# A block for rows beyond the experts' room, moved to the end of the program with a second pass of the MLP

## The chip, the core and the metric

The kernel runs on one core of a Trainium2 chip. A core has TensorE (PE, matmuls; its weight loads are listed as PEld), VectorE (DVE), ScalarE (ACT), GpSimd (POOL) and SyncE (SP), each with its own queue of instructions and its own sequencer, which handles register loads, branches and waits on semaphores. The metric is the device time of one execution in microseconds; of several runs the median counts.

## What is computed

Sliding-window attention, then a mixture of experts with one expert per token and a capacity, then a second MLP over all 1152 tokens:

```python
x = attention(q, k, v)                      # 2 x 576 tokens, 8 heads of 64, window of 64
x = x.transpose(0, 2, 1, 3).reshape(1152, 512)
# experts: token i goes to argmax(x @ w_gate), as long as that expert has room (288)
h = np.maximum(np.einsum('ecd,edf->ecf', disp, w1), 0.0)      # 8 experts, 512 -> 1024
y = np.einsum('ecf,efd->ecd', h, w2)                          # 1024 -> 512
x = gate_w * y[expert, pos]                                   # 0 where the expert was full
# second MLP
h = x @ w_in                                                  # 512 -> 2048
g = np.maximum(h, 0.0) + alpha * np.minimum(h, 0.0)
out = g @ w_out                                               # 2048 -> 512
```

## The kernel before

The kernel is written engine by engine in a fixed order (`tc.manual_schedule()`): what the program lists first on an engine stands first in its queue, and the framework adds the semaphore waits. All tensors of the matmuls are split into a high and a low part, and three matmuls (high x high, high x low, low x high) make one product (`mm3`, L185 to L188).

It has three stages. Attention, routing and the scatter of the rows by expert come first. Then the experts are worked off in an order that depends on how many rows each got: the rows lie sorted in `xs` (two tiles, high and low, 512 features as 4 blocks of 128 by 1152 + 256 columns), an expert of rank 1 to 3 gets a window of 256 rows (`wide_up`, `wide_down`), the others 128 (`narrow`), and the results go to `x2`, which is laid out like `xs`. The last expert is a wide one; its `wide_down` finishes the four feature blocks one after the other, and for each, `put(d)` has ScalarE write the high and VectorE the low part of that block of `x2` (L937, L938). The third stage is the second MLP, in four quarters `qq`. A quarter has 12 calls of `up` (each 12 matmuls of 384 columns into a tile `gps`, L188; ScalarE makes `u`, VectorE `g`, and both split it into `gh` and `gl`) and 9 of `down` (each 12 matmuls of 512 columns into `ops`, L1212, added to `acc` by ScalarE or VectorE). In the last quarter every `down` ends with a scatter of its 128 rows to `out` by GpSimd (L1220). The weights of this MLP come in through SyncE's queue (L92), in 32 pieces, and are converted and split by ScalarE and VectorE (`cvt_tick`), some of it ahead of the MLP, during the last expert.

Where an expert got more rows than its window holds, the rest is worked off between the experts and the second MLP. `n_over`, the number of such rows, is read into a register on every engine (L1098), and `with tc.If(n_over > 0)` (L1099) opens the block: it clears windows of `x2`, then holds for each of the eight experts a further `If` (L1120) with the whole of its two layers for the remaining rows. With the inputs of the runs shown `n_over` is 0, and all engines jump over the block. On TensorE the block is some 2370 of 4843 listed instructions. Behind the block, `over.close()` (L1160) gives the memory of `xs` free, and the pools of the second MLP open.

A `tc.If` has a branch for true and one for false on every engine. The false branch holds only semaphore steps, by which each engine's counters are raised to where the true branch would have left them, so that what stands behind the `If` can wait on one count in both cases.

The lines that touch the edge, as they stand:

```python
n_over = nc.values_load(inci[0:1, NS + 2 * NE:NS + 2 * NE + 1], min_val=0, max_val=NT)   # L1098
with tc.If(n_over > 0):                                                                    # L1099
    ...                                                                                    # L1101 to L1159
over.close()                                                                               # L1160
with ExitStack() as es:                                                                    # L1163, the second MLP
```

Of the kernel before, what the change touches and what calls it, by code (L numbers as in the profile page):

```python
# [27 lines left out]
def attention_moe_mlp_kernel(  # L28
# [145 lines left out]
    scattered, written = [], []  # L174
# [15 lines left out]
    with tc.manual_schedule():  # L190
# [905 lines left out]


        n_over = nc.values_load(inci[0:1, NS + 2 * NE:NS + 2 * NE + 1], min_val=0, max_val=NT)  # L1098
        with tc.If(n_over > 0):  # L1099
# [60 lines left out]
        over.close()  # L1160


        with ExitStack() as es:  # L1163
            accp = es.enter_context(tc.tile_pool(name="accp", bufs=1))
            gtp = es.enter_context(tc.tile_pool(name="gtp", bufs=4 * NTB))
            tmp = es.enter_context(tc.tile_pool(name="tmp", bufs=3))
            ps_h = es.enter_context(tc.tile_pool(name="ps_h2", bufs=4, space=PSUM))
            ps_o = es.enter_context(tc.tile_pool(name="ps_o", bufs=4, space=PSUM))
            acc = accp.tile([128, NTILE, D], F32, name="acc")
            base = 8 * NE  # L1170
            gts, unsplit = {}, []

            def need(c):
                while cvt_n[0] < 2 * (c - n_moe) + 3:
                    cvt_tick(c)

            def up(qq, c, tb, f):
                cs, fs = slice(TB * tb, TB * tb + TB), slice(128 * f, 128 * f + 128)
                ft = 4 * qq + 2 * c + f
                hi, lo = (w.rearrange("p (k f) -> p k f", k=4) for w in parts[base + 4 * qq + c])  # L1180
                need(base + 4 * qq + c)
                ps = ps_h.tile([128, TB], F32, name="gps", tag="g")
                for kk in range(4):
                    mm3(ps, (hi[:, kk, fs], lo[:, kk, fs]), (x2[0][:, kk, cs], x2[1][:, kk, cs]), kk == 0, kk == 3)
                u = tmp.tile([128, TB], F32, name="u", tag="u")
                g = tmp.tile([128, TB], F32, name="g", tag="gf")

                nc.scalar.activation(out=u, in_=ps, func=AF.Copy, scale=one[:, ft:ft + 1])  # L1188
                nc.vector.scalar_tensor_tensor(g, ps, slope[:, ft:ft + 1], u, op0=ALU.mult, op1=ALU.max)  # L1189
                split()  # L1190
                unsplit.append((tb, 2 * c + f, sign[:, ft:ft + 1], g))

            def split():

                while unsplit:
                    tb, f, sg, g = unsplit.pop()
                    gh = gtp.tile([128, TB], F32R, name="gh", tag="gh")
                    gl = gtp.tile([128, TB], F32R, name="gl", tag="gl")
                    nc.scalar.activation(out=gh, in_=g, func=AF.Copy, scale=sg)  # L1199
                    nc.vector.scalar_tensor_tensor(gl, g, sg, gh.bitcast(F32), op0=ALU.mult, op1=ALU.subtract)  # L1200
                    gts[tb, f] = (gh, gl)

            def down(qq, tt):
                tb, t = divmod(tt, TB // 128)
                ts_ = slice(128 * t, 128 * t + 128)
                need(base + 4 * qq + 3)
                ps = ps_o.tile([128, D], F32, name="ops", tag="o")
                for f in range(4):
                    hi, lo = (w.rearrange("p (k f) -> p k f", k=2) for w in parts[base + 4 * qq + 2 + f // 2])
                    gh, gl = gts[tb, f]  # L1210
                    for n, (a_, b_) in enumerate(((gh, hi), (gh, lo), (gl, hi))):
                        nc.tensor.matmul(ps, a_[:, ts_], b_[:, f % 2, :], start=f == 0 and n == 0,  # L1212
                                         stop=f == 3 and n == 2)
                sc = gate[:, tt:tt + 1]
                if qq == 0:
                    nc.scalar.mul(acc[:, tt, :], ps, sc)
                else:
                    nc.vector.scalar_tensor_tensor(acc[:, tt, :], ps, sc, acc[:, tt, :], op0=ALU.mult, op1=ALU.add)  # L1218
                if qq == NQ - 1:
                    ins = nc.gpsimd.indirect_dma_start(  # L1220
                        out=out[:, :],
                        out_offset=bass.IndirectOffsetOnAxis(ap=tok[:, tt:tt + 1].bitcast(U32), axis=0),
                        in_=acc[:, tt, :], in_offset=None)
                    apart(written, ins)


            sign, one, slope = (accp.tile([128, 16], F32, name=x) for x in ("sign", "one", "slope"))
            nc.vector.tensor_scalar(sign, al, 1.0, -2.0, op0=ALU.is_gt, op1=ALU.mult)
            nc.vector.tensor_scalar(sign, sign, 1.0, None, op0=ALU.add)
            nc.vector.tensor_scalar(one, sign, 1 / UP, None, op0=ALU.mult)  # L1230
            nc.vector.tensor_tensor(slope, one, al, op=ALU.mult)
            gate = accp.tile([128, NTILE], F32, name="gate")
            nc.vector.tensor_scalar(gate, gt[:, :, 1], 1 / UP, None, op0=ALU.mult)
            done = base - 1
# [57 lines left out]
```

## Time and profile before

| | us |
|---|---|
| median of 3 runs | 432.46 (432.07 to 435.01) |
| the profiled execution | 438.73 |
| its span, first to last instruction of the program | 437.0 |
| TensorE busy (matmuls) | 413.6 |
| VectorE busy | 322.6 |
| ScalarE busy | 225.9 |
| GpSimd busy | 62.8 |

Rows of the timeline give the start and the length in us, engine, line, operation and tiles, and in brackets the idle time ahead of the instruction and what ended it. A q behind an engine's name (PEq, DVEq, PEldq) is its sequencer: such steps occupy no engine. [...] In the rows of one line the three times after the count are shortest, median and longest, in ns, and behind them stand the starts of the first and the last, in us.

### The profile page before, as it was taken

The page shows a single profiled execution, that of the slowest core. Times are in us where ns is not written, and L with a number is a line of the kernel's source. Part 1 is how long each engine was busy: PE and PEld are TensorE (multiplying, and loading weights), DVE is VectorE, ACT ScalarE, POOL GpSimd, SP SyncE. Part 2 cuts the span into 40 slices and gives each one's busy share as a digit, 9 for nine tenths or more (in the row PEclk, how much of TensorE's full clock was granted, in tenths as well). Part 3 has the DMA queues.
Part 4 walks back from the last instruction along what each step waited for, and adds up shares of the span by engine and source line. Part 5 has one row for each costly group of instructions (what it writes and reads, how often), then busy time and mean ns, then how long its engine had stood idle before and what let it go on. Part 6 is the DMA issues. An engine that isn't in the chain of part 4 may idle for free. (4 is left out here: it accounts for less than half of the span.)

```text
span 437.0 us, 7987 instructions
## 1 busy us (share of the span) xinstructions
PE 413.6 (95%) x2707; PEld 374.4 (86%) x2707; DVE 322.6 (74%) x755; ACT 225.9 (52%) x474; POOL 62.8 (14%) x109
## 2 busy tenths in 40 slices
PE   7899979889999999999969999999999999999994
PEld 4789867578998899988969998899889998899883
DVE  3998958758988878877963996699994996245421
ACT  3887836455647654755533675577532770045200
POOL 8433535850000000000000000000000000000132
PEclk9999969999999999999996999999999999999998
DMA  7999676976698768788740345344341100000122
GB/s 254 303 355 382 209 244 243 371 208 187 211 316 262 247 239 303 231 273 284 230 164 4 103 137 145 96 145 115 128 144 48 49 0 1 0 2 0 37 99 82
DMA packets 27857, 74.90 MB, mean 171 GB/s; under 512 B 3041, under 2 KB 8161, under 8 KB 27809
## 3 DMA queue, kind: packets, MB, share of 16 engines
q1 hardware_dynamic: 25648, 67.08, 46.7%
q0 software_dynamic: 2160, 7.23, 4.6%
q8 instruction: 24, 0.39, 0.4%
q14 instruction: 25, 0.20, 0.2%
HBM read 62.75 MB, written 11.55 MB: 170 GB/s over the span
## 5 line engine op out<-in xcount | busy, mean ns | idle before, releaser
L106 DVE TENSOR_TENSOR wlo<-raw,whi 128x1024 fp32r<-128x1024 f32 x60 | 72.2, 1222 | 8.3 <-ACT whi L897 7.2
L188 PE MATMUL gps<-x2h,whi 128*128 128x384 f32 x192 | 65.5, 341 | 4.5 <-DVEq L1099 4.5
L188 PE MATMUL gps<-x2h,wlo 128*128 128x384 f32 x192 | 65.3, 340 | 0.0
L188 PE MATMUL gps<-x2l,whi 128*128 128x384 f32 x192 | 65.3, 340 | 0.0
L1188 ACT ACTIVATE u<-gps,one 128x384 f32<-128x384 f32 x48 | 27.7, 576 | 62.7 <-PE gps L188 62.7
L1212 PE MATMUL ops<-whi,gl 128*128 128x512 f32 x144 | 56.1, 390 | 0.0
L1212 PE MATMUL ops<-wlo,gh 128*128 128x512 f32 x144 | 56.1, 390 | 0.0
L1220 POOL DMA_INDIRECT out<-acc,tok x9 | 8.7, 965 | 329.4 <-DVE acc L1218 329.4
L1212 PE MATMUL ops<-whi,gh 128*128 128x512 f32 x144 | 56.0, 389 | 0.0
L897 ACT CAST whi<-raw 128x1024 fp32r<-128x1024 f32 x42 | 43.4, 1050 | 10.7 <-PE y L188 5.4
L1189 DVE SCALAR_TENSOR_TENSOR g<-gps,slope,u 128x384 f32<-128x384 f32 x48 | 29.5, 614 | 22.6 <-ACT u L1188 22.5
L1218 DVE SCALAR_TENSOR_TENSOR acc<-ops,gate,acc 128x512 f32<-128x512 f32 x27 | 20.0, 748 | 30.6 <-PE ops L1212 30.6
L188 PEld LDWEIGHTS gps<-x2h,whi 128*128 128x128 f32 x192 | 37.0, 193 | 4.8 <-ACTq L1099 4.6
L188 PEld LDWEIGHTS gps<-x2l,whi 128*128 128x128 f32 x192 | 36.9, 192 | 0.1
L188 PEld LDWEIGHTS gps<-x2h,wlo 128*128 128x128 f32 x192 | 36.9, 192 | 0.0
L1199 ACT ACTIVATE gh<-g,sign 128x384 fp32r<-128x384 f32 x48 | 29.3, 610 | 9.3 <-DVE g L1189 9.3
L371 ACT ACTIVATE pt<-ms,nm 128x128 f32<-128x128 f32 x72 | 28.0, 391 | 8.4 <-DVE nm L361 7.3
L1212 PEld LDWEIGHTS ops<-whi,gl 128*128 128x128 f32 x144 | 27.0, 188 | 5.6
L1212 PEld LDWEIGHTS ops<-wlo,gh 128*128 128x128 f32 x144 | 27.0, 188 | 5.6
L1212 PEld LDWEIGHTS ops<-whi,gh 128*128 128x128 f32 x144 | 27.0, 188 | 5.5
L1200 DVE SCALAR_TENSOR_TENSOR gl<-g,sign,gh 128x384 fp32r<-128x384 f32 x48 | 29.3, 610 | 0.2 <-ACT gh L1199 0.2
L158 DVE TENSOR_TENSOR wlo<-w,whi 128x512 fp32r<-128x512 f32 x32 | 22.0, 687 | 8.0 <-ACT whi L157 7.8
(247 smaller groups left out, 947.3 us busy)
## 6 DMA issues: line engine op xcount, KB each, us to landing
raw<-moe_in SPq DMA_DIRECT2D x61, 512.0 KB, 5.0
raw<-mlp_in SPq DMA_DIRECT2D x32, 512.0 KB, 3.6
xe<-zr SPq DMA_DIRECT2D x1, 6600.0 KB
v<-v_in SPq DMA_DIRECT2D x8, 512.0 KB
sw<-moe_in SPq DMA_DIRECT2D x4, 512.0 KB
qT<-q_in SPq DMA_DIRECT2D x4, 384.0 KB
kT<-k_in SPq DMA_DIRECT2D x4, 384.0 KB, 7.1
qT<-q_in SPq DMA_DIRECT2D x1, 768.0 KB, 9.5
```

Of the source, the lines that this page charges most:

```text
L106: eng.tensor_tensor(lo, raws.pop(c), hi.bitcast(F32), op=ALU.subtract)
L158: nc.vector.tensor_tensor(lo, w, hi.bitcast(F32), op=ALU.subtract)
L188: nc.tensor.matmul(ps, wa[i], xa[j], start=start and n == 0, stop=stop and n == 2)
L371: nc.scalar.activation(out=pt[:, p, :], in_=sc[:, p, :], func=AF.Exp, scale=-1.0, bias=nm[:, p:p + 1], accum_out=ss[:, p:p + 1])
L897: (nc.vector.tensor_copy if c % 4 == 3 else nc.scalar.copy)(ring_tiles(c)[0], raws[c])
L1188: nc.scalar.activation(out=u, in_=ps, func=AF.Copy, scale=one[:, ft:ft + 1])
L1189: nc.vector.scalar_tensor_tensor(g, ps, slope[:, ft:ft + 1], u, op0=ALU.mult, op1=ALU.max)
L1199: nc.scalar.activation(out=gh, in_=g, func=AF.Copy, scale=sg)
L1200: nc.vector.scalar_tensor_tensor(gl, g, sg, gh.bitcast(F32), op0=ALU.mult, op1=ALU.subtract)
L1212: nc.tensor.matmul(ps, a_[:, ts_], b_[:, f % 2, :], start=f == 0 and n == 0, stop=f == 3 and n == 2)
L1218: nc.vector.scalar_tensor_tensor(acc[:, tt, :], ps, sc, acc[:, tt, :], op0=ALU.mult, op1=ALU.add)
L1220: ins = nc.gpsimd.indirect_dma_start(out=out[:, :], out_offset=bass.IndirectOffsetOnAxis(ap=tok[:, tt:tt + 1].bitcast(U32), axis=0), in_=a ...
```

## The change

The block moves to the end of the program. `over.close()` comes directly behind the experts; the code of the second MLP becomes a function, `second_mlp`, that is called once in the place of the old code, and then once more as the last thing in the `If`, for the case that rows are left over. Since `xs` is gone by then, the block first gathers the rows again into two new tiles. The `If` gets `preferred_fallthrough_block=False`: the false branch stands directly behind the compare-and-branch in the program, and ends with an unconditional jump past the true branch to the program's closing barrier. Inside `up`, `need` is called ahead of looking the weights up, which in the first pass issues the same instructions.

```diff
-    scattered, written = [], []
+    scattered = []
...
                 else:
                     narrow(p, wins[p], xts.pop(p))
 
+        over.close()
+
+
+        def second_mlp():
+            written = []
+            with ExitStack() as es:
+                accp = es.enter_context(tc.tile_pool(name="accp", bufs=1))
...
+                def up(qq, c, tb, f):
+                    cs, fs = slice(TB * tb, TB * tb + TB), slice(128 * f, 128 * f + 128)
+                    ft = 4 * qq + 2 * c + f
+                    need(base + 4 * qq + c)
+                    hi, lo = (w.rearrange("p (k f) -> p k f", k=4) for w in parts[base + 4 * qq + c])
...
+        second_mlp()
+
+
 
         n_over = nc.values_load(inci[0:1, NS + 2 * NE:NS + 2 * NE + 1], min_val=0, max_val=NT)
-        with tc.If(n_over > 0):
+        with tc.If(n_over > 0, preferred_fallthrough_block=False):
+            over = ExitStack()
+            xsp = over.enter_context(tc.tile_pool(name="xsp2", bufs=1))
+            xs = [xsp.tile([128, 4, XW], F32R, name=f"xo{n}") for n in "hl"]
+            with ExitStack() as es:
+                gp = es.enter_context(tc.tile_pool(name="gp2", bufs=2))
+                ps_x = es.enter_context(tc.tile_pool(name="ps_x2", bufs=2, space=PSUM))
...
+                for j in range(NTILE):
+                    xg = gp.tile([128, ROW], F32, name="xgo", tag="xgo")
+                    nc.gpsimd.indirect_dma_start(
+                        out=xg, out_offset=None, in_=xe[:, :],
+                        in_offset=bass.IndirectOffsetOnAxis(ap=ixi[:, j:j + 1].bitcast(U32), axis=0))
...
             with ExitStack() as es:
                 zp = es.enter_context(tc.tile_pool(name="zp", bufs=1))
...
-        over.close()
-
-
-        with ExitStack() as es:
-            accp = es.enter_context(tc.tile_pool(name="accp", bufs=1))
...
+            over.close()
+            cvt_n[0] = 0
+            parts.clear()
+            for c in range(NRAW):
+                load(n_moe + c)
+            second_mlp()
```

On TensorE, before, this stands at the edge from the last matmuls of the experts (`y`, from the split hidden values `hh`, `hl` and the weights `whi`, `wlo`) to the block; in brackets are the semaphores that a row waits for, named after the engine or queue that raises them:

```order
L188 MATMUL y_3181<-hh,whi 128x256
L188 MATMUL y_3181<-hl,whi 128x256
L188 MATMUL y_3181<-hh,wlo 128x256
L1098 TENSOR_LOAD inci [waits DVE_49]
L1099 COMPARE_AND_BRANCH
L1111 TENSOR_LOAD at_z [waits DVE_49,PE_49,Activation_49]
```

And behind the block, where the second MLP begins with `gps`:

```order
L1120 UNCONDITIONAL_BRANCH [waits PE_49,PE_sequencer_49]
L1099 UNCONDITIONAL_BRANCH [waits PE_49,PE_sequencer_49]
L188 MATMUL gps<-x2h,whi 128x384 [waits DVE_49,PE_49,Activation_49]
L188 MATMUL gps<-x2l,whi 128x384
L188 MATMUL gps<-x2h,wlo 128x384
```

There the first matmul waits for three counts, those that the engines raise in the `If`. In the changed kernel the same place of TensorE reads as follows; the four feature blocks of the first `gps` repeat the three rows shown, each with its own two waits:

```order
L188 MATMUL y_3181<-hl,whi 128x256
L188 MATMUL y_3181<-hh,wlo 128x256
L188 MATMUL gps<-x2h,whi 128x384 [waits Activation_49]
L188 MATMUL gps<-x2l,whi 128x384 [waits DVE_49]
L188 MATMUL gps<-x2h,wlo 128x384
L188 MATMUL gps<-x2h,whi 128x384 [waits Activation_49]
```

The load and the branch are gone from between `y` and `gps`, and the counts waited for are those of the writes of `x2` by ScalarE (L937) and VectorE (L938), block by block. On all five engines the rows up to the end of the second MLP are otherwise the old ones in the old order.

GpSimd, before, reaches the `If` right behind its fills of `xs`, early in the expert stage. It passes over 25 listed rows, to the row of L1099 behind which the scatters stand:

```order
L1085 MEMSET xsl 128x4x256
L1098 TENSOR_LOAD inci [waits DVE_49]
L1099 COMPARE_AND_BRANCH
L1106 IOTA atf 128x9 [waits DVE_49,PE_49,Activation_49]
L1119 TENSOR_LOAD inci
```

In the changed kernel the `If` stands behind GpSimd's last scatter. The last rows of its way are these (`DMASW` are the semaphores that the scatters' transfers raise on landing; the row called ISA adds to them what the true branch would have added):

```order
L1159 DMA out<-acc,tok 1152x512 [waits DMASW2_49,DVE_49]
L183 MEMSET spacer 1x1 [waits Pool_49]
L1192 TENSOR_LOAD inci [waits DVE_49]
L1193 COMPARE_AND_BRANCH
L1193 ISA [waits Pool_49,Pool_sequencer_49,DMASW4_49,DMASW5_49,DMASW3_49,DMASW6_49,DMASW2_49,DMASW7_49,DMASW1_49,DMASW0_49]
L1193 UNCONDITIONAL_BRANCH
```

From that last jump it passes over 54 listed rows to the closing barrier. The other four engines pass 185 rows or more in either kernel: TensorE over 2300 before and over 3300 now.

## Rows read from the trace of the kernel before

**Rows 1.** Page: part 1 (busy us, share, instructions), clock line of part 2

```profile
PE 413.6 (95%) x2707; PEld 374.4 (86%) x2707; DVE 322.6 (74%) x755; ACT 225.9 (52%) x474; POOL 62.8 (14%) x109
...
PEclk9999969999999999999996999999999999999998
```

**Rows 2.** Stage table: stretch, length, busy time by engine, PEclk, DMA share, GB/s

```profile
216.00:225.50 9.50, 9.50 (x81) 9.50 (x81) 8.32 (x16) 4.40 (x9) 0.00 (x0) 1.00 0.62 207
...
230.20:236.20 6.00, 5.92 (x19) 5.95 (x20) 1.40 (x6) 0.58 (x1) 0.00 (x0) 0.50 0.01 1
236.20:257.00 20.80, 20.80 (x121) 20.80 (x120) 18.66 (x34) 14.76 (x28) 0.00 (x0) 1.00 0.33 94
...
282.40:307.30 24.90, 24.90 (x145) 24.86 (x144) 23.73 (x43) 17.96 (x33) 0.00 (x0) 1.00 0.42 128
...
431.30:437.00 5.70, 0.00 (x0) 0.00 (x0) 0.75 (x1) 0.00 (x0) 1.05 (x2) 0.76 0.22 82
```

**Rows 3.** Waits: who waited for whom, total us, times, longest us

```profile
PE gps L188 <- DVEq L1099: 4.5, 1, 4.5
```

**Rows 4.** Timeline, 225.3 to 236.5 us, the edge to the second MLP

```profile
225.53 0.28 PE L188 MATMUL y<-hh,wlo 128*128 128x256 f32 x1
...
225.86 0.82 DVE L938 TENSOR_TENSOR x2l<-y,x2h 128x256 f32 x2
...
230.28 0.66 PE L188 MATMUL gps<-x2h,whi 128*128 128x384 f32 x1 [4.47 <-DVEq L1099]
...
236.18 0.37 PE L188 MATMUL gps<-x2h,whi 128*128 128x384 f32 x1
```

**Rows 5.** The sequencers' steps of L1099 and, on GpSimd, L1098

```profile
L1099 PEldq EVENT_SEMAPHORE  x2: 51/51/51, 227.8 to 228.0; - x2
L1099 PEldq COMPARE_BRANCH  x1: 3840/3840/3840, 223.9 to 223.9; - x1
L1099 DVEq EVENT_SEMAPHORE  x2: 21/21/21, 230.1 to 230.2; - x2
L1099 DVEq COMPARE_BRANCH  x1: 72/72/72, 226.6 to 226.6; - x1
L1098 POOLq TENSOR_LOAD <-inci x1: 490/490/490, 84.5 to 84.5; - x1
L1099 POOLq EVENT_SEMAPHORE  x2: 17/17/17, 94.5 to 94.6; - x2
L1099 POOLq COMPARE_BRANCH  x1: 45/45/45, 85.0 to 85.0; - x1
```

**Rows 6.** DMA queues: two at 224 to 231 us, then all at 85 to 94

```profile
q8 instruction: 2, 0.03, 2.3%
q14 instruction: 6, 0.05, 2.1%
...
q0 software_dynamic: 582, 1.99, 73.5%
q1 hardware_dynamic: 136, 0.47, 12.8%
q8 instruction: 1, 0.02, 0.6%
```

**Rows 7.** Timeline, 425 to 437 us, the last eviction and the last scatter

```profile
431.30 0.75 DVE L1218 SCALAR_TENSOR_TENSOR acc<-ops,gate,acc 128x512 f32<-128x512 f32 x1 [1.97 <-PE ops L1212]
432.33 0.96 POOL L1220 DMA_INDIRECT out<-acc,tok  x1 [1.67 <-DVE acc L1218]
```

**Rows 8.** Steps of L1288 on SyncE (from 424.2 us) and GpSimd, and L1282

```profile
L1288 SPq EVENT_SEMAPHORE  x10: 28/28/10886, 424.2 to 436.0; - x10
L1288 POOLq EVENT_SEMAPHORE  x4: 17/17/17, 436.2 to 436.9; - x4
L1282 POOLq INC_SWDGE_SEM  x1: 31/31/31, 0.2 to 0.2; - x1
```

**Rows 9.** Timeline of GpSimd, 91 to 95 us

```profile
93.48 0.98 POOL L1085 MEMSET xsl<- 128x1024 f32 x1
```

More of the change, by code (lines that the diff above doesn't have):

```diff
@@ new lines, in attention_moe_mlp_kernel @@
+        second_mlp()
+        n_over = nc.values_load(inci[0:1, NS + 2 * NE:NS + 2 * NE + 1], min_val=0, max_val=NT)
+        with tc.If(n_over > 0, preferred_fallthrough_block=False):
[5 more added lines that the diff above has]
+                ps_x = es.enter_context(tc.tile_pool(name="ps_x2", bufs=2, space=PSUM))
+                for n in range(2):
+                    nc.gpsimd.memset(xs[n][:, :, NT:].bitcast(F32), 0.0)
+                for j in range(NTILE):
[3 more added lines that the diff above has]
+                        in_offset=bass.IndirectOffsetOnAxis(ap=ixi[:, j:j + 1].bitcast(U32), axis=0))
+                    tp = ps_x.tile([128, 4, 128], F32, name="xop", tag="xop")
+                    for kk in range(4):
+                        nc.tensor.transpose(tp[:, kk, :], xg[:, 128 * kk:128 * kk + 128], identf)
+                    cs = slice(128 * j, 128 * j + 128)
+                    nc.scalar.copy(xs[0][:, :, cs], tp)
+                    nc.vector.tensor_tensor(xs[1][:, :, cs], tp, xs[0][:, :, cs].bitcast(F32), op=ALU.subtract)
@@ L1159, in attention_moe_mlp_kernel @@
                                                 op=ALU.subtract)
-        over.close()
-        with ExitStack() as es:
-            accp = es.enter_context(tc.tile_pool(name="accp", bufs=1))
[L1165 to L1234, printed above, removed]
-            for qq in range(NQ):
-                for c in range(2):
-                    for n in range(2 * NTB):
-                        up(qq, c, *divmod(n, 2))
-                        if n in (1, 3, 5):
-                            cvt_tick(done)
-                    done += 1
-                split()
-                for tt in range(NTILE):
-                    down(qq, tt)
-                    if tt % 3:
-                        cvt_tick(done)
-                done += 2
```

70 lines of the change are left out of this document (added).

## The prediction

> **What bounds the kernel now.** I read the page's busy times first [rows 1]: the matmul side of TensorE is busy 413.6 of 437.0 us, VectorE 322.6. So only stretches in which TensorE stands or runs slowly are worth anything. The stage table then says where it is full [rows 2]: from 236.2 us on it is busy in all of every stretch that I asked for (20.80 of 20.80, 24.90 of 24.90), at granted clock 1.00; from 431.3 us on it does nothing: the last 5.7 us are VectorE's last eviction, the last scatter and the end of the program. The same table has one row at clock 0.50, 230.2 to 236.2 us, with 19 matmuls in 6 us where the next stretch places 121 in 20.8.
>
> The list of waits names what stands ahead of that row: TensorE's first matmul of the second MLP waited 4.5 us, and the releaser is VectorE's queue at L1099, the `If` [rows 3]. The timeline shows the edge [rows 4]: the last matmul of the experts starts at 225.53 us, the first of the second MLP at 230.28 and VectorE's last piece of x2 is done at 225.86 + 0.82 = 226.68, 3.6 us before that. No row of the overflow block stands between: it is jumped over. What the jump takes is in the sequencers' rows [rows 5]: TensorE's compare-and-branch lasts 3.84 us; VectorE's lasts 72 ns, but its next instruction comes at 230.1, 3.5 us after the branch at 226.6; VectorE's step at 230.1 is the one that TensorE waits for. While this goes on, the two queues that carry instructions move 2 and 6 packets [rows 6]: code at the far side of the jump is brought in.
>
> **What the change takes away.** The order of TensorE shows that the first `gps` matmuls now stand directly behind the last `y` matmul, and that the one wait for everything has become a wait per row block kk: for ScalarE's and VectorE's piece of x2 of that block alone. Are the pieces there? The `y` matmuls start every 0.12 us, so the first `gps` could start at 225.65. At full clock a 384-column matmul comes every 20.80 / 121 = 0.172 us [rows 2], three to a kk: kk = 2 reads the low half of x2 at 225.65 + 7 x 0.172 = 226.85, kk = 3 at 227.37. VectorE writes these two pieces at 225.86 to 226.27 and 226.27 to 226.68 [rows 4]. Both are there 0.6 us early, so I take no wait: **230.28 - 225.65 = 4.63 us**. If the matmuls did wait for the last piece, as they do behind the `If`, they would start at about 226.8 and the gain would be 3.5 us.
>
> The slow stretch hangs on the pause: the clock was 1.00 from 216.0 to 225.5 and is 0.50 in the row behind the pause [rows 2]. In it 18 matmuls start, from 230.28 until the nineteenth at 236.18 [rows 4], in 5.90 us; at full clock they take 18 x 0.172 = 3.10. With TensorE busy through the edge I take full clock: **2.80 us**. The other end is 0, if the clock falls anyway.
>
> Would TensorE then wait for others? The second MLP's first quarter gets its evictions and weight splits from VectorE and ScalarE, and it now meets them at full speed from the start. The second quarter already does that: in 282.4 to 307.3 VectorE is busy 23.73 of 24.90 us and TensorE still 24.90 [rows 2]. VectorE enters the first quarter with nothing left over (five small constants of about 0.2 us each). I cost this at nothing; the cover is VectorE's 24.90 - 23.73 = 1.2 us of slack there, and each microsecond of work beyond it would be one of TensorE's.
>
> On every engine the executed instructions are otherwise the same ones in the same order; loads of the second MLP's weights move past SyncE's load and branch, which now stand behind all of them.
>
> **What it adds.** The load of `n_over`, the branch and the jump now stand at the end, and the jump still has to pass the block, which is longer: on all five engines, to reach the closing barrier. Each engine's cost counts only so far as it comes later than what closed the program before. That was the last scatter: it starts at 432.33; SyncE's long wait, which began at 424.2 and took 10.886, ended at 435.1; nine short waits follow until 436.0 (0.1 us each), and GpSimd's side of the barrier comes at 436.2 [rows 7, 8]. In the old kernel's times:
> - TensorE is done at 431.3 and needs 3.9 us for the jump: 435.2. Hidden, by 0.8 us.
> - VectorE ends at 431.30 + 0.75 = 432.05, plus 3.5: 435.6. Hidden, by 0.4 us.
> - ScalarE and SyncE finish their work earlier, and jump earlier.
> - GpSimd must, as its order shows, wait for all scatters to land ahead of its last two steps in the short branch (an addition to the scatters' semaphores, then the jump). Its 0.49 us register load [rows 5] is hidden under the landing. The addition takes 31 ns where it stands at the program's start [rows 8]. SyncE's run of waits needs those semaphores and so starts behind it.
>
> Two or three short steps ahead of SyncE's run are 0.1 to 0.4 us, the whole run once more would be 0.9; I take **+0.4 us**, if GpSimd's jump itself brings in no code. It passes 54 listed rows. In the old kernel GpSimd jumped over 25 rows at 85.0, and in 85 to 94 us only one instruction packet moves, on q8 and none on q14 [rows 6]; the q8 packets are about twice as large (0.03 MB in 2, against 0.05 in 6), and at the jump of the four others both queues moved. I read q8 as TensorE's alone, so that GpSimd's jump brought nothing in. The jumps that did pass 185 rows or more; this one is nearer to the short one. If it is not free it costs what VectorE's did: GpSimd is at the barrier at 435.1 + 0.3 + 3.5 = 438.9 in place of 436.2, +2.7 us.
>
> [...]
>
> **The sum.** The profiled execution took 438.73 us, 437.0 of it the span. 438.73 - 4.63 - 2.80 + 0.4 = 431.7 us. The median of the three runs is 432.46, 6.27 below the profiled one; I assume the edge costs the same there and take the difference of 7.03 over: **425.4 us**.
>
> **The rivals.**
> 1. *The speed does not come back.* The pause goes, but the clock still falls to half somewhere near 226 us, or the runs without the profiler never paid for it: 432.46 - 4.63 + 0.4 = 428.2. For it: the clock line of the page dips in one more place, its sixth slice of 10.9 us [rows 1], so that this edge is not its only cause. Against: every stretch in which TensorE is full and was full before is at 1.00 [rows 2]. Chance 0.10.
> 2. *The jump is paid at the end by GpSimd.* 432.46 - 7.43 + 2.7 = 427.7. For it: the target is farther than in the old jump. Against: no q14 packet at the old one. Chance 0.13.
> 3. *The change does not do what it says:* something else keeps TensorE at the edge (code that must be brought in anyway, a wait for released memory), and only the place of the branch differs: 432.46 + 0.4 = 432.9. Against: the waits in the order name only pieces of x2. Chance 0.04.
> 4. *Slower.* GpSimd's jump takes what its rows in the old kernel show at face value: branch at 85.0, next step at 94.5 [rows 5], 9.5 us. Then it reaches the barrier at 435.1 + 0.3 + 9.5 = 444.9, 8.7 us late: 432.46 - 7.43 + 8.7 = 433.7. It decides against the change from 7.4 us up. Against: GpSimd's own queue was busy with fills until 93.48 + 0.98 = 94.46 [rows 9] and the step behind the branch waits for them. Chance 0.03.
>
> **How the numbers follow.** The forecast has chance 0.70; its own range is 424.2 to 426.6: at the lower end the tail costs nothing (425.0) and both kernels' medians are off by the 0.4 us that lie between the median and the fastest run of before; at the upper end the matmuls wait for the last piece of x2 (a gain of 3.5 in place of 4.63). Rivals 1 and 2 reach to 428.2, and I end the range there, since rivals 3 and 4 hold only 0.07: 424.2 to 428.2. About 1% (4.3 us) is what a measurement of this kernel can tell, its three runs lying 432.07 to 435.01. The forecast, most of rival 2 and a part of rival 1 are beyond it: faster 0.82. Rivals 3 and 4 lie within 1%, as do the rest of 1 and 2: same 0.15. Slower by over 1% needs a tail worse than rival 4: 0.03.
>
> **What would show it.** Right: no wait of TensorE at the first `gps`, the x2l row of VectorE ending ahead of the eleventh `gps` matmul; granted clock 1.00 through that edge; the last scatter 7.4 us earlier; long branches on TensorE and VectorE at the end, inside the landing of the last scatter. Wrong: a gap of a microsecond or more at the edge; a row at 0.50 behind it; GpSimd's closing steps over 3 us after the landing.

## The result, and the profile after

The changed kernel takes **430.73 us** (median of 20 runs) against **435.43 us** for the kernel before (20 runs beside it): ratio 0.9897, 95% interval 0.9869 to 0.9925, that is 3.3 to 5.7 us less. The ratio leaves out one run of the changed kernel, 458.32 us at a mean granted clock of 0.84. The forecast was 425.4 us, in a range up to 428.2. It missed twice: the time expected to be saved was 7.03 us and 4.70 were (the difference of the medians), and the 432.46 us that it started from, a median of three runs, lay 3.0 below the median of twenty.

The changed kernel's profiled run took 430.24 us, its span 428.5. What stands ahead of the edge happened to take 3.9 us less there than in the profiled run of before (the last `y` starts at 221.63 us against 225.53 [rows 4]; the dip in the page's clock line between 55 and 75 us is less deep, 8 tenths where it was 6); the runs of both kernels scatter by some microseconds (before: 431.60 to 437.78), so I compare from the edge onwards. First the busy times and the clock line of the page:

```profile
PE 407.8 (95%) x2707; PEld 369.6 (86%) x2707; DVE 323.1 (75%) x755; ACT 225.9 (53%) x474; POOL 61.2 (14%) x109
...
PEclk9999998999999999999999999999999999999997
```

The dip in the middle of the clock line, to 6 tenths in [rows 1], is gone. The timeline at the edge and at the end (start, length, engine, line, operation and tiles):

```profile
221.63 0.28 PE L188 MATMUL y<-hh,wlo 128*128 128x256 f32 x1
...
221.75 0.34 PE L188 MATMUL gps<-x2h,whi 128*128 128x384 f32 x1
...
221.96 0.82 DVE L938 TENSOR_TENSOR x2l<-y,x2h 128x256 f32 x2
...
419.96 0.75 DVE L1157 SCALAR_TENSOR_TENSOR acc<-ops,gate,acc 128x512 f32<-128x512 f32 x1 [1.97 <-PE ops L1151]
420.99 0.96 POOL L1159 DMA_INDIRECT out<-acc,tok  x1 [1.67 <-DVEq L1193]
421.95 0.09 POOL L183 MEMSET spacer<- 1x1 f32 x1
```

The first `gps` starts 0.12 us behind the last `y`, with no idle time in brackets; before it was 4.75 [rows 4]. From the first `gps` to the last eviction it is 419.96 - 221.75 = 198.21 us, before 431.30 - 230.28 = 201.02 [rows 4, 7]. The stage table (columns as in [rows 2]; in brackets the instructions, PEclk as a share of full speed) has no row at half speed behind the edge any more:

```profile
216.00:225.50 9.50, 9.50 (x72) 9.50 (x71) 7.52 (x18) 3.64 (x8) 0.00 (x0) 1.00 0.49 160
225.50:236.00 10.50, 10.50 (x63) 10.50 (x62) 9.13 (x17) 7.59 (x15) 0.00 (x0) 1.00 0.24 71
```

The end is another matter. From the last scatter's start to the end of the span it was 437.0 - 432.33 = 4.7 us [rows 7]; it is 428.5 - 420.99 = 7.5. The sequencers' steps there (L1193 is the `If`, L1319 the program's closing barrier; shortest, median, longest in ns, then the starts of the first and the last):

```profile
L1193 PEldq COMPARE_BRANCH  x2: 93/1767/3441, 416.1 to 420.3; - x2
L1193 DVEq COMPARE_BRANCH  x2: 51/56/60, 420.6 to 421.0; - x2
L1193 POOLq EVENT_SEMAPHORE  x2: 43/818/1592, 422.4 to 424.1; - x2
L1193 POOLq INC_SWDGE_SEM  x1: 719/719/719, 424.1 to 424.1; - x1
L1193 POOLq COMPARE_BRANCH  x1: 38/38/38, 424.9 to 424.9; - x1
L1319 SPq EVENT_SEMAPHORE  x12: 28/28/28, 424.8 to 425.5; - x12
L1319 POOLq DRAIN  x1: 2331/2331/2331, 425.4 to 425.4; - x1
```

TensorE's jump takes 3.44 us and is over at 423.7, inside the landing, as forecast; VectorE branches at 421.0 and has its next step at 424.1, 0.1 us past it. GpSimd waits until 424.0 for the scatters to land, adds to their semaphores (0.72 us), branches at 424.9, and at 425.4 begins a DRAIN of 2.33 us (a step of that name stands in every engine's closing barrier; those of the other four take 80 ns at most). SyncE is through with its waits at 425.5. So the program then waits 2.2 us for GpSimd's DRAIN alone, which ends at 427.7; the span ends 0.8 later.

Such a DRAIN stood in the kernel before too, in the closing barrier (L1288), under other work:

```profile
L1288 POOLq DRAIN  x1: 4092/4092/4092, 432.1 to 432.1; - x1
```

It began while GpSimd's last operations were still to come, and ended at 436.2, 2.8 us behind the last of them (433.38: the scatter of [rows 7] and a fill of 0.09 us after it), and again 0.8 us ahead of the end. SyncE had its last wait at 436.0 [rows 8]. So landing (SyncE's long wait is over at 435.1 [rows 8]) and DRAIN ran side by side, and SyncE's run of waits was through 0.2 us before DRAIN.

### The profile page after: what moved, and what is told of

It is laid out like the page before. It is cut to its first block, busy times and chain, and to the rows that moved or that the text cites. A ratio compares the mean times of both kernels' runs of the same rounds, so it can differ in the third digit from the quotient of the medians.

```text
span 428.5 us, 7975 instructions
## 1 busy us (share of the span) xinstructions
PE 407.8 (95%) x2707; PEld 369.6 (86%) x2707; DVE 323.1 (75%) x755; ACT 225.9 (53%) x474; POOL 61.2 (14%) x109
## 5 line engine op out<-in xcount | busy, mean ns | idle before, releaser
L188 PE MATMUL gps<-x2h,wlo 128*128 128x384 f32 x192 | 64.2, 334 | 0.0
L188 PE MATMUL gps<-x2h,whi 128*128 128x384 f32 x192 | 64.2, 334 | 0.0
L188 PE MATMUL gps<-x2l,whi 128*128 128x384 f32 x192 | 64.2, 334 | 0.0
L188 PEld LDWEIGHTS gps<-x2h,whi 128*128 128x128 f32 x192 | 36.1, 188 | 0.1
L188 PEld LDWEIGHTS gps<-x2h,wlo 128*128 128x128 f32 x192 | 36.0, 188 | 0.0
```

The lines of the kernel that those rows point to most:

```text
L188: nc.tensor.matmul(ps, wa[i], xa[j], start=start and n == 0, stop=stop and n == 2)
```

## The experiments

The first four ran on one chip (before: 434.68 us), e5 to e8 on a second (436.52), e9 to e12 on a third (437.75). What was to be told apart: is the gain at the edge whole, and what at the end took 2.8 us back: code that GpSimd's jump brings in (the second rival of the prediction), the step on the scatters' semaphores, or the DRAIN?

**e1_no_block.** The changed kernel without the load of `n_over`, the `If` and the block (it leaves out the work for rows beyond the room, of which these inputs have none).

```diff
-        n_over = nc.values_load(inci[0:1, ...], min_val=0, max_val=NT)
-        with tc.If(n_over > 0, preferred_fallthrough_block=False):
-            ...
```

> The changed kernel without the block and its If; the rows beyond the experts' room are left out (there are none with these inputs). What is left is the edge alone, without the jump at the end. If the edge gave 7.4 us and the end took 2.8 back (from the start of the last scatter to the end of the span 4.7 us before, 7.5 after), this kernel has the edge of the changed one and the end of the old one: 4.7 us behind the last scatter, about 7.4 us (1.7%) faster than before, ratio 0.983. Rival: the edge is worth less in most runs (about 4.5 us, as the changed kernel's ratio of 0.990 taken alone would say) and the end costs nothing: ratio 0.990.

Measured: 426.33 us, ratio 0.9789 (0.9736 to 0.9841). The span is 424.5, the last scatter starts at 419.88, so the end is 4.6 us again. Its DRAIN:

```profile
L1232 POOLq DRAIN  x3: 40/108/4090, 419.6 to 424.3; - x3
```

The first and longest of the three ends 2.8 us behind GpSimd's last operation (420.93), as in the kernel before. Between the medians it is 8.4 us, and the 7.4 of the edge lie inside the interval, which does not reach the changed kernel's (0.9869 to 0.9925). So the edge gives what it should, and what is missing lies at the end.

**e2_no_indirect.** The changed kernel with no indirect DMA of GpSimd in the block: fills in place of the gathers, no scatter in the second pass (both stand in the block that is jumped over, so rows left over would not be worked off). The false branch then has nothing to add to the scatters' semaphores and does not wait for them.

```diff
-                    nc.gpsimd.indirect_dma_start(
-                        out=xg, out_offset=None, in_=xe[:, :],
-                        in_offset=bass.IndirectOffsetOnAxis(ap=ixi[:, j:j + 1].bitcast(U32), axis=0))
+                    nc.gpsimd.memset(xg, 0.0)
...
-                    if qq == NQ - 1:
+                    if qq == NQ - 1 and put:
```

> The changed kernel with a block that is as long on TensorE, VectorE, ScalarE and SyncE, but holds no indirect DMA of GpSimd: the gathers are replaced by fills and the second pass scatters nothing, so the block would not give the reference's rows if it ran. In the false branch GpSimd then neither waits for the scatters to land nor adds to their semaphores. If it is the steps behind the landing that cost (whether the jump or the drain), they now lie under the landing: 4.7 to 5.1 us behind the last scatter, ratio 0.983. Rival: the jumps of TensorE and VectorE past a long block are what the end waits for: 7.5 us as in the changed kernel, ratio 0.990.

Measured: 428.64 us, ratio 0.9875 (0.9817 to 0.9933); last scatter at 419.76, end of the span 424.9, 5.1 us later. The long block still stands at the end and GpSimd still jumps over it; only the wait and the step are gone:

```profile
L1317 POOLq DRAIN  x1: 2602/2602/2602, 421.5 to 421.5; - x1
```

DRAIN takes 2.6 us all the same, also without the addition ahead of it, but now it starts at 421.5, while the last scatter is on its way, and costs nearly nothing. So the jump is not what costs, and neither does DRAIN by being there: it costs by starting late. This rests on the profile; the interval of the ratio holds the 0.983 of the theory and the 0.990 of the rival.

**e3_short_end** and **e4_long_on_gpsimd.** The block at the end cut to eight gathers (again the work for left-over rows is left out), so that the wait and the step stay and every jump is short; and the same with 300 fills on GpSimd, so that its jump alone is long.

```diff
         with tc.If(n_over > 0, preferred_fallthrough_block=False):
-            over = ExitStack()
-            ...
+            with tc.tile_pool(name="gp2", bufs=1) as gp:
+                xg = gp.tile([128, ROW], F32, name="xgo")
+                for j in range(8):
                     nc.gpsimd.indirect_dma_start(...)
+                for _ in range(300):          # e4 alone
+                    nc.gpsimd.memset(xg, 0.0)
```

> The changed kernel with a short block at the end: eight gathers of GpSimd and nothing else, the rest of the block is left out. GpSimd still waits for all scatters to land and adds to their semaphores, but the jump of every engine is a few instructions long. First theory (GpSimd's jump brings in code): the steps behind the landing shrink, 5.5 to 6 us behind the last scatter and a closing drain of GpSimd well under 1 us. Second theory (the addition to the semaphores leaves GpSimd's queue busy, which the closing drain waits for): as in the changed kernel, a drain of 2.3 us, 7.4 us behind the last scatter, ratio 0.990.

> The same short block with 300 fills of GpSimd behind the eight gathers, so that GpSimd alone has a long jump, longer than in the changed kernel; the rest of the block is left out. First theory (the jump brings in code): 2.8 us or more above the kernel with the short block, 8 to 8.5 us behind the last scatter. Second theory (the addition and the drain): code also has to come for a jump that is that long, so up to 3 us are added between branch and drain, and the drain of 2.3 us becomes shorter where it runs beside that. If drain and jump simply follow one another: 10 us behind the last scatter.

Measured: e3 428.0 us, ratio 0.9832 (0.9767 to 0.9896), last scatter to end 7.4 us (420.24 to 427.6); e4 431.4, ratio 0.992 (0.9883 to 0.9957), 9.35 us (419.15 to 428.5). GpSimd's closing steps of e3:

```profile
L1193 POOLq INC_SWDGE_SEM  x1: 715/715/715, 423.1 to 423.1; - x1
L1193 POOLq COMPARE_BRANCH  x1: 38/38/38, 423.9 to 423.9; - x1
...
L1240 POOLq DRAIN  x1: 2272/2272/2272, 424.0 to 424.0; - x1
```

And of e4:

```profile
L1193 POOLq INC_SWDGE_SEM  x1: 719/719/719, 422.0 to 422.0; - x1
L1193 POOLq COMPARE_BRANCH  x1: 41/41/41, 422.8 to 422.8; - x1
...
L1242 POOLq DRAIN  x1: 2352/2352/2352, 425.3 to 425.3; - x1
```

The instruction queue of e4 in 421 to 428 us (packets, MB, share of 16 engines):

```profile
q14 instruction: 2, 0.02, 0.6%
```

One of the two moves between e4's branch and its DRAIN; between branch and DRAIN of e3 and of the changed kernel none does. With a short jump DRAIN follows the branch after 0.1 us, with a long one after 2.5 us; in the changed kernel it is 0.5. DRAIN takes 2.3 us in all three. So the long jump of GpSimd costs 2.5 us here, about what the second rival took for it (that the time goes into bringing in code is my reading of that one packet), but the changed kernel's jump is not such a one. My theory up to e3 had been that it is; it falls. DRAIN and jump are two prices, one behind the other.

The spans show a little less of this than the steps: in e3 DRAIN ends 6.0 us behind the last scatter's start, in the changed kernel 6.7, but in e3 the span ends 1.3 us later still, not 0.8. And the medians do not follow the ends to the microsecond: e3, with the longer end, lies 0.6 us below e2. Their intervals overlap widely, so what the steps at the end cost is read from the profiles.

**e5_late_two.** The changed kernel with its last two scatters behind the block, from a small tile of their own, so that GpSimd's wait, step and branch lie beside TensorE's last matmuls. The computation is whole. In the block a tile is cut to the columns that are used, to make room.

```diff
+                    elif qq == NQ - 1 and tt >= NTILE - LATE:
+                        nc.vector.scalar_tensor_tensor(fin[:, tt - NTILE + LATE, :], ps, sc, acc[:, tt, :], op0=ALU.mult, op1=ALU.add)
...
             second_mlp()
 
+        for tt in range(NTILE - LATE, NTILE):
+            every.append(scatter_out(fin[:, tt - NTILE + LATE, :], tt, every[:]))
```

> The changed kernel with the last two tiles' results in a small tile of their own, and their two scatters behind the block instead of ahead of it (the tile of gathered inputs inside the block is cut to the columns that are used, so that it all fits; the computation is whole). Theory (GpSimd's closing DRAIN takes 2.3 to 2.8 us whenever it comes after indirect DMAs, and costs only where nothing covers it): the wait for the first seven scatters' landing, the 0.72 us INC_SWDGE_SEM and the branch now lie beside TensorE's last work, the two last scatters start up to some 1.1 us later than in the change, and the span ends about 4.7 us behind the last one instead of 7.5, with DRAIN beside the landing again: some 1.7 us below the change, ratio about 0.985 to 0.986 to the kernel before. Rival (the two steps are paid wherever the block stands, since GpSimd waits at the branch for the others): last scatter to end about 7 us, ratio 0.99 or above.

Measured: 431.01 us, ratio 0.9873 (0.9815 to 0.9932), a little above the 0.986 expected; from the last scatter's start to the end of the span 429.5 - 424.48 = 5.0 us. The interval holds the changed kernel's 0.9897 too, so the comparison was made again on one chip (e12 below).

**e6_short_block_old_place.** The kernel before, block at the old place, its body cut to two instructions.

```diff
         with tc.If(n_over > 0):
-            ...
+            nc.vector.memset(x2[0][0:1, 0, NT:NT + 1].bitcast(F32), 0.0)
+            nc.scalar.copy(x2[1][0:1, 0, NT:NT + 1], x2[0][0:1, 0, NT:NT + 1].bitcast(F32))
```

> The kernel before with the block at its old place, its body cut to two instructions on one element, one of VectorE and one of ScalarE (it leaves out the whole work for rows beyond the room, which these inputs do not have). Theory (the pause at the edge is code that must be brought in for a branch past a long body): first matmul of the second MLP about 1.3 us behind the last y matmul instead of 4.5, the granted clock stays at 1.00 behind it, last scatter to end as before (4.7): about 5.9 us less, ratio about 0.986. Rival (the branch itself or the wait for VectorE's count costs the pause, however long the body): pause 4.5 us, ratio 1.00.

Measured: 428.52 us, ratio 0.9836 (0.9773 to 0.9899). The first `gps` comes 0.12 us behind the last `y` (223.79 and 223.67), not the 1.3 expected, and the matmuls keep full pace behind it: the `gps` ones all take 0.33 to 0.35 us, where before the slow ones took 0.52. TensorE's branch is there, and short:

```profile
L1099 PEldq COMPARE_BRANCH  x1: 230/230/230, 222.1 to 222.1; - x1
```

It takes 0.23 us in place of 3.84 [rows 5], and lies beside the last matmuls, ahead of which the sequencer runs (by 1.6 us: branch at 222.1, last `y` at 223.67). But TensorE has no work in this block, so it has no count to raise behind the branch and nothing there to wait for; e9 gives it one.

**e7_matmuls_in_pause.** The kernel before with 18 matmuls ahead of the `If`, into a tile that nobody reads.

```diff
+            idle = ps_x.tile([128, 512], F32, name="idle2", tag="x")
+            fw = parts[8 * NE][0]
+            for _ in range(18):
+                nc.tensor.matmul(idle, fw[:, :128], fw[:, :512], start=True, stop=True)
```

> The kernel before with 18 matmuls of 512 columns ahead of the branch, on a filter chunk that is loaded already and into a tile that nobody reads, so that TensorE works while the others branch. Theory (the slower clock of the second MLP's first part follows from TensorE standing still at the edge): the last 18 end about 4 us behind the last y matmul, and if TensorE's own branch still takes 3.8 us behind them the pause stays and the kernel is 4 us slower (ratio 1.009, clock falls as before); if its code comes in while they run, the second MLP starts about as late as before but at clock 1.00, 2.8 us less, ratio 0.994. Rival (the clock falls there whatever TensorE did): late start and clock below 1.00, ratio 1.00 or above.

Measured: 436.3 us, ratio 0.9994 (0.9957 to 1.0031). TensorE's first `gps` in the timeline:

```profile
226.48 0.41 PE L188 MATMUL gps<-x2h,whi 128*128 128x384 f32 x1 [1.41 <-DVEq L1103]
```

Its branch in the sequencer's steps:

```profile
L1103 PEldq COMPARE_BRANCH  x1: 4788/4788/4788, 221.2 to 221.2; - x1
```

And the stage behind it:

```profile
226.40:236.40 10.00, 9.92 (x57) 9.96 (x58) 6.20 (x15) 5.01 (x10) 0.00 (x0) 1.00 0.09 26
```

The 18 matmuls run until 225.07 and cover all but 0.9 us of TensorE's branch; 1.41 us of pause are left, ended by VectorE's step, and the clock stays at 1.00 behind it. The first `gps` is 5.80 us behind the last `y` (220.68) in place of 4.75; against 2.80 for the clock that would be 1.75 us less, ratio 0.996. The interval holds that as well as 1.00, so the time does not settle it; the clock's row does.

**e8_fallthrough_only.** The kernel before with `preferred_fallthrough_block=False` and nothing else.

```diff
-        with tc.If(n_over > 0):
+        with tc.If(n_over > 0, preferred_fallthrough_block=False):
```

> The kernel before with the one argument of the branch that the change also sets (preferred_fallthrough_block=False), and the block at its old place. Theory: the argument is worth nothing by itself, the pause at the edge stays at 4.5 us, ratio 1.00. Rival (the argument decides which way is laid out behind the branch, so the pause goes by it alone): pause of 1 us or less, ratio about 0.985.

Measured: 437.28 us, ratio 0.9989 (0.9941 to 1.0037). TensorE's wait at the edge:

```profile
PE gps L188 <- issue: 5.0, 1, 5.0
```

Its branch:

```profile
L1099 PEldq COMPARE_BRANCH  x2: 93/2292/4491, 223.8 to 226.1; - x2
```

And the stage behind it:

```profile
230.60:236.00 5.40, 5.27 (x19) 5.30 (x20) 1.10 (x6) 0.58 (x1) 0.00 (x0) 0.60 0.03 9
```

The pause is there as before, and half speed follows it, if for a shorter time: by my estimate (a mean of 0.60 over 5.4 us, if the clock is 0.50 or 1.00) the matmuls are back at full pace some 4 us behind the first `gps`, before it took 5.9 [rows 4]. The argument is worth nothing by itself; the place of the block is.

**e9_short_block_matmul.** e6 with one matmul more in the block, so that TensorE has a count to raise in the false branch.

```diff
+            with tc.tile_pool(name="psi", bufs=1, space=PSUM) as psi:
+                idle = psi.tile([128, 512], F32, name="idle2")
+                fw = parts[8 * NE][0]
+                nc.tensor.matmul(idle, fw[:, :128], fw[:, :512], start=True, stop=True)
```

> The kernel of e6 with one matmul more in the short block at the old place, so that TensorE too has the branch (in e6 it had no step there at all; as there, the work for rows beyond the room is left out). Theory (the 4.5 us are code brought in past a long body; a branch with a near target costs only the wait for the slowest engine): TensorE waits for VectorE, whose last piece of x2 ends some 1.0 us behind the last y matmul and whose branch and step take 0.2 to 0.3 us more, so the first matmul of the second MLP comes 1.2 to 1.5 us behind the last y matmul; clock 1.00 behind it; about 6 us less than before, ratio 0.986. Rival (branching on TensorE costs microseconds by itself): pause 4 us or more, ratio 1.00.

(The expectation's remark that TensorE had no step in e6 was too strong: it had the branch, shown above, and no step behind it.) Measured: 431.73 us, ratio 0.985 (0.9809 to 0.989), as expected. The edge in the timeline:

```profile
227.80 0.28 PE L188 MATMUL y<-hh,wlo 128*128 128x256 f32 x1
228.38 0.41 PE L188 MATMUL gps<-x2h,whi 128*128 128x384 f32 x1 [0.30 <-PEq L1099]
```

TensorE's branch:

```profile
L1099 PEldq COMPARE_BRANCH  x1: 227/227/227, 226.2 to 226.2; - x1
```

VectorE's branch and its next step:

```profile
L1099 DVEq COMPARE_BRANCH  x1: 72/72/72, 228.9 to 228.9; - x1
L1099 DVEq EVENT_SEMAPHORE  x1: 21/21/21, 229.1 to 229.1; - x1
```

And the stage behind it:

```profile
228.50:238.50 10.00, 10.00 (x58) 10.00 (x59) 6.83 (x18) 5.19 (x10) 0.00 (x0) 1.00 0.27 78
```

TensorE's branch takes 0.23 us again, VectorE's jump 0.2 in place of 3.5 [rows 5]. At the same place the long body makes the jump dear, and the short one does not. The pause is 0.30 us, shorter than expected, and what ends it is TensorE's own step behind the branch, not VectorE's. So the short block takes a second thing away: it writes nothing that `gps` reads, and the wait for VectorE's step is gone with it. Had that wait stood, the first `gps` would have come no sooner than 229.1, some 1.3 us behind the last `y` as expected, still far from 4.75.

**e10_plain_out.** The changed kernel with SyncE writing the nine result tiles in sorted order instead of GpSimd's scatters, so that the rows are not in their places.

```diff
+                    if qq == NQ - 1 and not put:
+                        nc.sync.dma_start(out[128 * tt:128 * tt + 128, :], acc[:, tt, :])
...
-        second_mlp()
+        second_mlp(False)
```

> The changed kernel with the nine scatters of the first pass replaced by plain writes of SyncE to rows in sorted order (so the output's rows are not in their places). GpSimd's last indirect DMA is then one of the routing, over 300 us before the end; INC_SWDGE_SEM and the branch stay. Theory A (DRAIN is long only when indirect DMAs were issued shortly before): DRAIN about 0.2 us as at the program's start, INC_SWDGE_SEM possibly 0.03. Theory B (DRAIN costs 2.3 us once any indirect DMA has been issued in the program): 2.3 to 2.8 us again, INC_SWDGE_SEM 0.7. Either way last row of VectorE to the end under 7 us.

Measured: 433.37 us in a single run, span 431.7. GpSimd had nothing left to do and went through branch and DRAIN in the expert stage already; its steps, and SyncE's in the closing barrier (L1321):

```profile
L1195 POOLq INC_SWDGE_SEM  x1: 540/540/540, 95.6 to 95.6; - x1
...
L1321 POOLq DRAIN  x1: 1615/1615/1615, 96.6 to 96.6; - x1
...
L1321 SPq EVENT_SEMAPHORE  x13: 17/28/28, 430.0 to 431.0; - x13
```

So it came soon after the routing's gathers (the last began at 91.66 us) and not 300 us later: the two theories are not told apart. DRAIN took 1.6 us there. The end is no shorter, 8.4 us from the last eviction's start (423.31) and not the 7 at most that were expected, since now SyncE branches at 427.4 and has its next step at 430.0: its own jump over the block, 2.6 us, ended last.

**e11_changed_again** and **e12_late_two_again.** The changed kernel and e5 once more, side by side.

> The changed kernel itself, beside the next one on the same chip: 4.5 us below the kernel before, ratio 0.990 as measured, last matmul to the end 8.6 us.

> The kernel of e5 beside the changed kernel on the same chip, since in e5 they could only be compared through the kernel before. Theory (its tail is 1.2 us shorter from the last matmul on, 7.4 against 8.6 us): 1.2 us below e11. Rival (it gains nothing): the two medians within 0.5 us, or e12 above.

Measured: 434.97 us, ratio 0.9919 (0.9888 to 0.9951), and 432.58 us, ratio 0.9871 (0.9829 to 0.9913): the late scatters are 2.4 us better in the medians, with intervals that just overlap. From the last eviction's start to the end of the span the profiles give 433.6 - 424.97 = 8.6 us for e11 and 431.2 - 424.14 = 7.1 for e12, some 1.6 less. GpSimd's timeline at the end of e12:

```profile
425.23 0.96 POOL L1105 DMA_INDIRECT out<-fin,tok  x1 [4.45 <-DVEq L1203]
...
426.49 0.96 POOL L1105 DMA_INDIRECT out<-fin,tok  x1 [0.21 <-issue]
427.45 0.09 POOL L183 MEMSET spacer<- 1x1 f32 x1
```

Its sequencer's steps (L1203 is the `If`, L1332 the closing barrier):

```profile
L1203 POOLq INC_SWDGE_SEM  x1: 680/680/680, 422.5 to 422.5; - x1
...
L1332 POOLq DRAIN  x3: 40/113/4035, 426.3 to 430.9; - x3
```

The step on the semaphores is done at 423.2, ahead of the last eviction; the first and longest DRAIN ends 2.8 us behind the last operation again. What is paid for it: both scatters wait for VectorE's branch (the 4.45 us name L1203), so the last one starts 2.35 us behind the last eviction's start, before it was 1.03 [rows 7].

## Why the prediction was right and wrong, point by point

**The pause: right.** 4.63 us expected, 4.75 - 0.12 = 4.63 gone. The last low piece of `x2` ended at 222.78, ahead of the `gps` matmul that reads it (the eleventh, at 223.49), so no wait was left (the forecast's own range had that case at 3.5 us). That the jump is dear past the long body and not past a short one is shown by e9 and e8: same place, short body, 0.23 us for TensorE's branch; same body, other layout, 4.49 (before: 3.84).

**The clock: right.** 2.80 us expected, 201.02 - 198.21 = 2.81 gone. The first rival (the speed does not come back) falls. In the profiles of before and of e8, with pauses of 4.5 and 5.0 us, the clock is at half behind the edge (0.50 over 6.0 us, 0.60 over 5.4); in those of the changed kernel, e7 and e9, with pauses of 0 to 1.4 us, at full. How long the half speed lasts varies, as e8 shows, so the 2.80 are the price in one run. From the last `y` to the last scatter it was 432.33 - 225.53 = 206.80 us and is 420.99 - 221.63 = 199.36: the 7.4 that the forecast named.

**No engine in the way in the first quarter: right.** TensorE is busy in all of 225.5 to 236.0 (10.50 of 10.50 us).

**The jumps of TensorE and VectorE at the end: right.** They are covered by the landing and GpSimd's steps behind it (TensorE done at 423.7, landing at 424.0, VectorE's next step at 424.1).

**The tail: wrong, and this is the step of the reasoning that failed.** The prediction took "two or three short steps ahead of SyncE's run", 0.1 to 0.4 us, with 31 ns for the addition [rows 8], and +0.4. It was 7.51 - 4.67 = +2.84. Two things were mis-sized:

- The addition takes 0.72 us behind the scatters, not 31 ns. The row of 31 ns is from the start of the program, with no indirect DMA before it; it is the same operation with nothing ahead of it.
- What closes the program was read as SyncE's run of waits. GpSimd's DRAIN was in the same list as the rows of [rows 8], was left out, and is what comes last. Before, it began just ahead of the last operations and took until 2.8 us behind them, for the most part beside the landing. In the changed kernel it can't begin until the landing is over: 2.0 us of landing behind GpSimd's last operation (422.04), 1.4 for step and branch, then 2.33 of DRAIN, in all 5.7 in place of 2.8. The change put a wait for the landing ahead of a piece of work that had run beside it. One of the prediction's own signs of being wrong came true with it: GpSimd's closing steps end 427.7 - 424.0 = 3.7 us after the landing.

**The second rival** had the price (+2.7) and not the cause. GpSimd's jump takes 0.5 us at most; e3 shows the tail long (7.4 us) with a short jump (0.1 us), e4 what a long one would have added (2.5 us). This kernel's jump on GpSimd is none of the long ones, and its 0.5 us decide. The third and fourth rivals fall too: nothing holds TensorE at the edge, and the jump does not take 9.5 us.

**The sum.** With the measured tail, 4.63 + 2.81 - 2.84 = 4.60 us, against 4.70 between the medians. That is closer than the evidence can tell (the terms are from one profile of each kernel, the interval is 3.3 to 5.7 us), but no further term is called for.

**The base: wrong too.** The three runs shown (432.07 to 435.01) were low: their median stood 3.0 us under that of twenty. This alone would have carried the time out of the range, if only just: with the forecast's own saving, 435.43 - 7.03 = 428.4. The tail alone would not have: from the old base, 432.46 - 4.60 = 427.9. That is near the second rival's 427.7 without its cause. The chance given for faster by over 1% was 0.82; the ratio of 0.9897 lies on that bound. The range took 0.4 us for both kernels' medians, from the distance between the median and the fastest of three; the highest of the three, 2.6 above the median, would have been the better measure.

**What stays open.** What GpSimd does in the 2.3 us of DRAIN. It takes 2.3 to 2.6 us behind scatters, also where all of them have landed (the changed kernel, e3, e4), 1.6 behind the gathers of the routing (e10); what sets the length was not separated.

## What to carry to other kernels

A block that is hardly ever run cost its jump where it stood, here 4.63 us of pause and 2.81 us at half speed behind it: move such a block off the busy engine's path, and then follow every engine from its last operation to the barrier, semaphore steps and DRAIN included, and ask of each what it now has to wait for before it may begin. A false branch that waits for transfers serialized here what had run beside them, and the tail grew by 2.84 us; putting the branch ahead of the last transfers (e12) gave back about half of that, 1.6 us in the profiles. And a duration from a row holds for the state it was read in (the step on the semaphores: 31 ns at the program's start, 0.72 us behind scatters): take it from a place where the same things went before.

## What the runs showed of the hardware that I had not expected

- GpSimd's closing DRAIN took 2.3 us after scatters even when all of them had landed (2331 ns in the changed kernel, begun 1.4 us after the landing), 2.6 with the last one on its way (e2). The span ended 0.8 us behind it in both kernels and in e1, e2, e4, e11 and e12, in e3 1.3.
- INC_SWDGE_SEM took 0.68 to 0.72 us behind scatters (the changed kernel, e3, e4, e12), 0.54 behind gathers (e10), against 31 ns at the program's start [rows 8].
- A branch with a near target cost TensorE nothing where its false branch has no step (e6: 0.12 us from `y` to `gps`): its sequencer took the branch at 222.1, 1.6 us ahead of the last `y`. Where it has one, it was 0.58 us from `y` to `gps`, 0.30 of them idle (e9).
- A jump past long code took 2.5 us on GpSimd (e4), 2.6 on SyncE (e10) and 3.4 to 4.8 on TensorE (the changed kernel, e8, e7), a short one 0.1 and 0.2 us on GpSimd (e3) and TensorE (e9).
